# A retention layer and its gated unit: query blocks kept four tokens per partition, and another order in the first slots

## The chip, the cores and the metric

The kernel runs on one core of a Trainium2 chip. The metric is the time of one execution on the device in microseconds (us). The core has five engines that each work through their own list of instructions: TensorE (PE; its weight loads are shown as PEld), VectorE (DVE), ScalarE (ACT), GpSimd (POOL) and SyncE (SP), which issues nearly all transfers (DMA). An engine that waits for a semaphore holds up all that stands behind it in its list.

## The reference

```python
# attention-like part, B, H, S, D = 8, 8, 576, 64
scores = scale * np.matmul(q, k.transpose(0, 1, 3, 2))
Dmat = np.where(rel >= 0, gamma[:, None, None] ** rel[None, :, :], 0.0)   # rel = pos_i - pos_j
x = np.matmul(scores * Dmat[None], v)            # then heads side by side: [B, S, 512]
# gated part, K = 5
gate_pre = sum over k of conv_w[k] * xp[:, k:k + S, :]      # causal, along the tokens
gate = 1.0 / (1.0 + np.exp(-gate_pre))
out = (gate * (x @ w_val)) @ w_out
```

Inputs and output are float32.

## The kernel before

The decay gamma^(i-j) is split into a factor of the key's token and one of the query's. So the work runs in chunks of 128 tokens of one batch, all heads at once: scores of the chunk against itself under a causal mask, plus a state carried from the chunks before it. A batch has four such chunks and a tail of 64 tokens; two tails make one chunk. In all there are 36 chunks: 16 of batches 0 to 3, two of their tails, then the same for batches 4 to 7.

Lines 426 to 483 are a software pipeline written out by hand, a loop over slots t from -2 to 37. Slot t holds work of several chunks and emits it in a fixed order on every engine: the loads of chunk t+6; the casts to bf16 of chunk t+4 (keys `kb`, values `vb`, POOL) and of the query blocks to be turned in slot t+2 (`qb`, POOL); `take_state(t)` (ACT); `scores(t+1)` (PE) and the two `masks` (DVE, from PSUM to `p0`, `p1`); `values(t)` (PE); `take_x(t)` (DVE, L310), which multiplies the result `o` in PSUM by the query factor `gout` and writes it to `xg` in SBUF; `turn_k(t+2)`, four transposes on PE into the one PSUM tile `tps`, copied out by DVE as `kt`; `turn_q`, the same for queries, copied out by ACT (L244); and `carried(t+1)` and `update(t+1)`, the products with the state and into it.

Two chunks make a unit n of the gated part. In slot 2n+2 stand `conv(n)` (40 matmuls, L362), its sigmoid (ACT) and `value(n, .)`; in slot 2n+3 `project(n, .)`, whose output ACT copies (L390) and SP sends out (L393, L396). So a convolution marks the start of every even slot from slot 2 on.

Queries come in two forms. For batches 0 and 1 (`FIRST = 2`) and for the tails, each chunk's queries are a transfer of their own (`fqc`, 256 KB). For batches 2 to 7 one transfer of 1 MB brings all 512 queries of a batch with four consecutive tokens in each partition (`fqb`), which gives runs of 1 KB in HBM where the others have 256 bytes. Such a batch is turned in four blocks r = 0 to 3: block r holds tokens r, r+4, r+8 and so on. L240 puts the tokens back in order, by writing the block with a step of four elements into `qtb`. A table (L400 to L420) says in which slot which block is turned and when a batch's block is loaded.

SP issues in program order, so an output that isn't ready holds up the loads behind it. The loads of chunks 0 to 5 and the weights stand ahead of the loop (L99 to L111).

Of the kernel before, what the change touches and what calls it, by code (L numbers as in the profile page):

```python
# [13 lines left out]
F32 = mybir.dt.float32  # L14
# [7 lines left out]
def kernel(  # L22
# [22 lines left out]
    FIRST = 2  # L45
# [26 lines left out]
    with tc.manual_schedule():  # L72
# [13 lines left out]
        def load(t):  # L86
            kind, b, c = chunks[t]
            load_one("k", k, kind, b, c, LA + 1)
            if kind == "tail" or b < FIRST:
                load_one("q", q, kind, b, c, LA)  # L90
            load_one("v", v, kind, b, c, LA + 1)
# [9 lines left out]
        load(0)  # L101
# [8 lines left out]
        for t in range(3, LA - 2):  # L110
            load(t)  # L111
# [19 lines left out]

        tok = consts.tile([P, NCH + 1], F32, name="tok")
# [15 lines left out]
        warm = consts.tile([P, 1], F32, name="warm")  # L148
        nc.scalar.activation(warm, lsc, AF.Sigmoid)
# [4 lines left out]
        for t in sbd + sbl:  # L154
            nc.vector.memset(t, 0.0)
        xg = [xp.tile([P, GB, NP, PAD + S], BF16, name=f"xg{g}") for g in range(B // GB)]
# [24 lines left out]
        def prep_wv():  # L181

            src = wvf.rearrange("p o (pr ab hl j) -> p o pr ab hl j", pr=2, ab=2, hl=2)
            for (blk, j0, ab, hl) in ((0, 0, 0, 0), (0, 64, 1, 0), (2, 0, 1, 1), (2, 64, 0, 1)):
                nc.scalar.copy(wvb[:, :, blk:blk + 2, j0:j0 + 64], src[:, :, :, ab, hl, :])

        def prep_wo(o):
            nc.vector.tensor_copy(wob[:, o], wof[:, o])


        bf = {}

        def cast_kv(t):
            kind, b, c = chunks[t]
            kb = bfp.tile([P, H, D], BF16, name="kb")
            vb = bfp.tile([P, H, D], BF16, name="vb")
            (nc.vector if t < 2 else nc.gpsimd).tensor_copy(kb, loaded["k", kind, b, c])  # L197
            nc.gpsimd.tensor_tensor(vb, loaded["v", kind, b, c],  # L198
                                    gin[:, c, :].unsqueeze(2).to_broadcast([P, H, D]), op=ALU.mult)
            bf[t] = (kb, vb)  # L200
# [4 lines left out]
        def cast_q(job):  # L205
            qb = bfp.tile([P, H, D], BF16, name="qb")
            if job[0] == "own":
                kind, b, c = chunks[job[1]]
                src = loaded["q", kind, b, c]
            else:  # L210
                src = loaded["qb", job[1]][:, :, job[2], :]
            nc.gpsimd.tensor_copy(qb, src)  # L212
            qbf[job] = qb

        def turned(src):
            ps = ps_t.tile([P, NP, P], BF16, name="tps")
# [7 lines left out]
        def turn_k(t):  # L224
            ps = turned(bf[t][0])
# [4 lines left out]
        def turn_q(job, eng=None):  # L230
            ps = turned(qbf[job])
# [281 lines left out]
```

## Time and profile before

| | us |
|---|---|
| three runs | 186.19, 186.20, 213.15 |
| median | 186.2 |
| the profiled execution | 186.13 |
| its span (first to last instruction) | 184.1 |
| busy PE, DVE, ACT, POOL | 150.5, 116.3, 104.6, 79.8 |
| bytes moved, HBM read and written | 30.42 MB, 9.44 MB |

The rows in the next sections come from one profiled execution. The slices give each engine's busy share of a fortieth of the span (4.6 us) in tenths. A row of a timeline has the start, the duration, the engine, the line, the operation with output and inputs, how many instructions were merged (x) and, in brackets, how long the engine was idle before it and what ended that. A row of groups has the count, the busy time, the mean duration in ns, and the idle time before the group with what ended most of it. A row of windows has for each engine the busy time in that stretch, then TensorE's granted clock, the share of busy DMA engines (which can exceed 1, since transfers of several packets are counted while they are open) and the rate in GB/s. A piece of the chain of waits is a start, a length and what ran.

### The profile page before, as it was taken

The numbers are of one execution on the slowest core, as the hardware profiler recorded it, in microseconds if no ns is written. First come the engines' busy times: TensorE is split into PE (matmuls) and PEld (weight loads), VectorE is DVE, ScalarE is ACT, GpSimd is POOL, SyncE is SP. The second block draws the span as 40 slices with busy tenths as digits, with TensorE's granted clock in tenths as the row PEclk, the third lists the DMA queues.
The fourth block names the chain that finished last, engine by engine and source line by source line (L and its number), as shares of the span: only waits on it lengthen the run. The fifth ranks groups of instructions, "written<-read, shape, count | busy, mean of one in ns | idle before, by whom it ended". The sixth has DMA issues, their size and how long they took to land.

```text
span 184.1 us, 5545 instructions
## 1 busy us (share of the span) xinstructions
PE 150.5 (82%) x2255; PEld 113.1 (61%) x2273; DVE 116.3 (63%) x227; ACT 104.6 (57%) x182; POOL 79.8 (43%) x118
## 2 busy tenths in 40 slices
PE   0172529059999999999999999999999999999960
PEld 0151416046768686777868677686867768677630
DVE  7364527016576677777677876767787678876320
ACT  6606203206876786686755668687766764455330
POOL 4333041088684347632575157443684451710000
PEclk9999999859999999999999999999999999999997
DMA  6997999989999999999999899999999987923215
GB/s 134 219 304 183 220 218 220 306 187 251 213 270 276 251 256 237 242 230 227 249 255 270 232 237 279 255 214 231 252 271 221 240 219 174 270 80 116 76 39 116
DMA packets 100199, 40.21 MB, mean 218 GB/s; under 512 B 88378, under 2 KB 94542, under 8 KB 100174
## 3 DMA queue, kind: packets, MB, share of 16 engines
q1 hardware_dynamic: 100144, 39.86, 91.3%
q8 instruction: 17, 0.28, 0.7%
q14 instruction: 8, 0.07, 0.1%
q10 hardware_dynamic: 30, 0.01, 0.0%
HBM read 30.42 MB, written 9.44 MB: 217 GB/s over the span
## 4 chain that ended last, share of the span: by engine, by line
PE 61%; SPq 17%; DVE 7%; ACT 7%; DMA 3%; issue 2%; POOL 0%; DVEq 0%; ACTq 0%
PE g L387 16%; PE g L377 15%; SPq L79 14%; PE g L362 11%; PE tps L219 8%; ACT qtb L244 6%; DVE p L269 5%; PE s L260 5%; PE o L301 4%; DMA fqc<-in_q_dram 3%; DVE z L380 3%; PE st L329 2%; SPq L109 1%; PE o L284 1%; SPq L95 1%
## 5 line engine op out<-in xcount | busy, mean ns | idle before, releaser
L269 DVE TENSOR_TENSOR p<-s,mask 128x512 bf16<-128x512 f32 x64 | 43.9, 685 | 16.2 <-PE s L260 15.1
L198 POOL TENSOR_TENSOR vb<-fvc,gin 128x512 bf16<-128x512 f32 x36 | 37.5, 1042 | 14.1 <-DMA fvc<-in_v_dram 10.6
L377 PE MATMUL g<-xg,wvb 128*128 128x256 bf16 x288 | 38.1, 278 | 0.0
L380 DVE TENSOR_TENSOR z<-gate,g 128x512 bf16<-128x512 f32 x36 | 24.7, 687 | 20.3 <-PE g L377 20.3
L390 ACT COPY ob<-g 128x512 f32<-128x512 f32 x36 | 22.2, 618 | 24.6 <-PE g L387 24.6
L244 ACT COPY qtb<-tps 128x512 bf16<-128x512 bf16 x24 | 31.5, 1314 | 5.0 <-PE tps L219 5.0
L387 PE MATMUL g<-wob,z 128*128 128x512 bf16 x126 | 32.9, 379 | 1.4 <-DVE z L380 0.5
L197 POOL CAST kb<-fkc 128x512 bf16<-128x512 f32 x34 | 20.8, 613 | 28.3 <-DMA fkc<-in_k_dram 15.5
L219 PE MATMUL tps<-ident,kb 128*128 128x128 bf16 x144 | 15.3, 233 | 20.4 <-POOL kb L197 14.7
L377 PEld LDWEIGHTS <-wvb 128*128 128x128 bf16 x288 | 27.4, 100 | 3.4 <-issue 0.4
L370 ACT ACTIVATE gate<-g 128x512 f32<-128x512 f32 x36 | 19.5, 595 | 14.0 <-PE g L362 14.0
L227 DVE COPY kt<-tps 128x512 bf16<-128x512 bf16 x36 | 15.3, 424 | 16.7 <-PE tps L219 16.5
L219 PEld LDWEIGHTS <-kb 128*128 128x128 bf16 x144 | 8.9, 102 | 25.8 <-POOL kb L197 15.5
L362 PE MATMUL g<-xg,dg 64*64 64x256 bf16 x720 | 24.2, 279 | 0.0
L310 DVE TENSOR_TENSOR xg<-o,gout 128x512 bf16<-128x512 f32 x32 | 21.8, 680 | 0.0
L362 PEld LDWEIGHTS <-dg 64*64 64x64 bf16 x720 | 19.0, 109 | 2.3 <-issue 0.6
L212 POOL CAST qb<-fqc 128x512 bf16<-128x512 f32 x12 | 7.3, 610 | 30.1 <-DMA fqc<-in_q_dram 28.4
L340 ACT CAST sbd<-st 64x256 bf16<-64x256 f32 x48 | 17.8, 371 | 2.7 <-PE st L329 2.2
L387 PEld LDWEIGHTS <-z 128*128 128x128 bf16 x144 | 12.6, 98 | 10.3 <-DVE z L380 1.2
L212 POOL CAST qb<-fqb 128x512 bf16<-128x512 f32 x24 | 14.6, 610 | 8.5 <-DMA fqb<-in_q_dram 8.4
L219 PE MATMUL tps<-ident,qb 128*128 128x128 bf16 x144 | 14.9, 231 | 2.0 <-DVE kt L227 1.6
L244 ACT COPY qt<-tps 128x512 bf16<-128x512 bf16 x10 | 5.9, 588 | 17.9 <-PE tps L219 17.9
(52 smaller groups left out, 139.6 us busy)
## 6 DMA issues: line engine op xcount, KB each, us to landing
fkc<-in_k_dram SPq DMA_DIRECT2D x32, 256.0 KB, 5.2
fvc<-in_v_dram SPq DMA_DIRECT2D x32, 256.0 KB, 5.5
out_dram<-ob SPq DMA_DIRECT2D x32, 256.0 KB, 3.7
fqb<-in_q_dram SPq DMA_DIRECT2D x6, 1024.0 KB, 7.9
fqc<-in_q_dram SPq DMA_DIRECT2D x8, 256.0 KB, 6.4
wvf<-in_moe_w_val_dram SPq DMA_DIRECT2D x1, 1024.0 KB, 8.4
wof<-in_moe_w_out_dram SPq DMA_DIRECT2D x4, 256.0 KB, 4.8
fkc<-in_k_dram SPq DMA_DIRECT2D x8, 128.0 KB, 3.6
```

Source lines behind the costliest of these rows:

```text
L79: nc.sync.dma_start(out=t, in_=src[b, :, c * P:(c + 1) * P, :].rearrange("h p d -> p h d"))
L198: nc.gpsimd.tensor_tensor(vb, loaded["v", kind, b, c], gin[:, c, :].unsqueeze(2).to_broadcast([P, H, D]), op=ALU.mult)
L212: nc.gpsimd.tensor_copy(qb, src)
L219: nc.tensor.transpose(ps[:, pr, :], flat[:, pr * P:(pr + 1) * P], ident)
L244: nc.scalar.copy(dst, ps)
L269: nc.vector.tensor_tensor(p, sps[t][i], m.unsqueeze(1).to_broadcast([P, NP, P]), op=ALU.mult)
L310: nc.vector.tensor_tensor(x[:, bl, :, PAD + i0:PAD + i0 + P], ops[t], gout[:, :, i0:i0 + P], op=ALU.mult)
L362: nc.tensor.matmul(g[bank][cols, pr, :], lhsT=dg[rows, blk, kk, :], rhs=xs(n, rows, blk, kk), start=(pr == 0 and kk == 0), stop=(pr == 1 a ...
L377: nc.tensor.matmul(vps[:, j, :], lhsT=wvb[:, o, 2 * i + j, :], rhs=xs(n, slice(0, P), o, PAD), start=(j == 0 and o == 0), stop=(j == 1 and ...
L380: nc.vector.tensor_tensor(z, gsb[n][i], vps, op=ALU.mult)
L387: nc.tensor.matmul(o, lhsT=zsb[n, j // 2][:, j % 2, i * P:(i + 1) * P], rhs=wob[:, j, :], start=(j == 0), stop=(j == NP - 1))
L390: nc.scalar.copy(ob, o)
```

## The change

All eight batches now take the form with four tokens per partition, and the step of four is no longer undone when the queries are copied out of PSUM. `qtb` keeps the blocks side by side, `[P, NP, RQ, P]`. A chunk's 128 queries are then 32 columns of each of the four blocks, so that the columns of the scores and of `o` stand in the order (r, n) for token 4n + r. Three places answer to that: `queries` returns the four runs of 32, the mask is copied once with its columns in that order (`mask_q`), and `take_x` reads `o` with a step of 32 columns to write `xg` in token order.

```diff
-                    qtd["batch", b] = tp_sb.tile([P, NP, RQ * P], BF16, name="qtb", bufs=2)
-                dst = qtd["batch", b].rearrange("p o (n r) -> p o r n", r=RQ)[:, :, r, :]
+                    qtd["batch", b] = tp_sb.tile([P, NP, RQ, P], BF16, name="qtb", bufs=2)
+                dst = qtd["batch", b][:, :, r, :]
...
+    def queries(t, rows, pr):
+        if kind == "tail":
+            return qtd["own", t][rows, pr, :]
+        return qtd["batch", b][rows, pr, :, c * P // RQ:(c + 1) * P // RQ]
...
+        nc.gpsimd.tensor_copy(mask_q.rearrange("p (r n) -> p n r", r=RQ), mask.rearrange("p (n r) -> p n r", r=RQ))
...
-                nc.vector.tensor_tensor(x[:, bl, :, PAD + i0:PAD + i0 + P], ops[t], gout[:, :, i0:i0 + P], op=ALU.mult)
+                by_token = lambda a: a.rearrange("p o (n r) -> p o n r", r=RQ)
+                nc.vector.tensor_tensor(by_token(x[:, bl, :, PAD + i0:PAD + i0 + P]),
+                                        ops[t].rearrange("p o (r n) -> p o n r", r=RQ),
+                                        by_token(gout[:, :, i0:i0 + P]), op=ALU.mult)
```

The rest reorders the first slots. Batch 0's block is loaded right after chunk 0's keys, batch 1's after chunk 3. Batch 0 is cast (POOL and DVE in turn) and turned in slot -2, batch 1 as a whole in slot 2, batch 2 from slot 3 on, one block a slot. Keys are cast in slot t for chunk t+3, values for t+2, query blocks for slot t+1. In slots 1 to 3 `turn_k` and `turn_q` come after the value products and projections, and ACT and DVE copy the turned blocks in turn. The weight casts move: half of `w_val` to POOL (slot -1), half to ACT in slot 1; `w_out` to ACT and DVE at the end of slot 2. The memsets of `sbl` and the load of the sigmoid table move into slot -2. At the end one of the last four output transfers is issued by ACT.

```diff
-        load(0)
+        load_one("k", k, *chunks[0], LA + 1)
+        load_queries(0)
+        load_one("v", v, *chunks[0], LA + 1)
         load(1)
...
-        for t in range(3, LA - 2):
+        load(3)
+        load_queries(1)
+        for t in range(4, LA - 2):
             load(t)
...
-            for job in qjobs.get(t + 2, []):
+            if ok(t + 2) and t == -1:
+                cast_k(t + 2)
+            if ok(t + 2):
+                cast_v(t + 2)
+            if t == -1:
+                prep_wv(g_copy, 0)
+            if ok(t + 3):
+                cast_k(t + 3)
+            for job in qjobs.get(t + 1, []):
                 cast_q(job)
-            if ok(t + 4):
-                cast_kv(t + 4)
...
+            if ok(t + 2) and 1 <= t <= 3:
+                turn_k(t + 2)
+                for i, job in enumerate(jobs):
+                    turn_q(job, v_copy if i % 2 else s_copy)
...
-                    nc.sync.dma_start(out=out[b + 2 * i + j, NCH * P:S, :], in_=ob[j * TAIL:(j + 1) * TAIL])
+                    (nc.scalar if last and j else nc.sync).dma_start(out=out[b + 2 * i + j, NCH * P:S, :], in_=ob[j * TAIL:(j + 1) * TAIL])
```

On SP, the queue of the loads, from the keys of chunk 4 to those of chunk 7 (fkc keys, fqc a chunk's queries, fvc values, fqb a batch's queries; the numbers are buffers). Before:

```order
L79 DMA fkc_129<-in_k_dram 128x8x64
L79 DMA fqc_131<-in_q_dram 128x8x64
L79 DMA fvc_133<-in_v_dram 128x8x64
L79 DMA fkc_135<-in_k_dram 128x8x64
L79 DMA fqc_137<-in_q_dram 128x8x64
L79 DMA fvc_139<-in_v_dram 128x8x64
L95 DMA fqb_290<-in_q_dram 128x8x256
L79 DMA fkc_292<-in_k_dram 128x8x64
L79 DMA fqc_294<-in_q_dram 128x8x64
L79 DMA fvc_296<-in_v_dram 128x8x64
L95 DMA fqb_358<-in_q_dram 128x8x256
L79 DMA fkc_360<-in_k_dram 128x8x64
```

And after, the same stretch with batch 1's block ahead of it:

```order
L94 DMA fqb_123<-in_q_dram 128x8x256
L78 DMA fkc_125<-in_k_dram 128x8x64
L78 DMA fvc_127<-in_v_dram 128x8x64
L78 DMA fkc_129<-in_k_dram 128x8x64
L78 DMA fvc_131<-in_v_dram 128x8x64
L94 DMA fqb_287<-in_q_dram 128x8x256
L78 DMA fkc_289<-in_k_dram 128x8x64
L78 DMA fvc_291<-in_v_dram 128x8x64
L94 DMA fqb_340<-in_q_dram 128x8x256
L78 DMA fkc_342<-in_k_dram 128x8x64
```

The reads of 256 KB for queries are gone from the stretch; batch 1's block stands ahead of chunk 4, and the blocks of batches 2 and 3 (fqb_287, fqb_340) stand where they stood.

On POOL, from the casts of chunk 4 on (kb, vb, qb the cast keys, values and queries). Before:

```order
L212 CAST qb_298<-fqc_131 128x512
L212 CAST qb_300<-fqb_290 128x512
L197 CAST kb_302<-fkc_129 128x512
L198 TENSOR_TENSOR vb_303<-fvc_133,gin_164 128x512
L212 CAST qb_366<-fqc_137 128x512
L212 CAST qb_368<-fqb_290 128x512
L197 CAST kb_370<-fkc_135 128x512
```

And after:

```order
L197 CAST kb_348<-fkc_125 128x512
L215 CAST qb_350<-fqb_123 128x512
L215 CAST qb_352<-fqb_123 128x512
L215 CAST qb_354<-fqb_123 128x512
L215 CAST qb_356<-fqb_123 128x512
L202 TENSOR_TENSOR vb_405<-fvc_127,gin_158 128x512
L197 CAST kb_407<-fkc_129 128x512
L215 CAST qb_409<-fqb_287 128x512
L497 COPY maskt_192<-mask_150 128x128
L498 MEMSET maskt_192 64x64
L202 TENSOR_TENSOR vb_555<-fvc_131,gin_158 128x512
L197 CAST kb_557<-fkc_289 128x512
```

The first cast of batch 2's block stood ahead of chunk 4's keys (kb_302) and now stands behind chunk 5's (kb_407), ahead of chunk 5's values and chunk 6's keys. The four casts of batch 1's block stand between the keys and the values of chunk 4.

More of the change, by code (lines that the diff above doesn't have):

```diff
@@ L266, in masks @@
         def masks(t, i):
-            m = mask if chunks[t][0] == "full" else mask_t
+            m = mask_q if chunks[t][0] == "full" else mask_t
             p = pp.tile([P, NP, P], BF16, name=f"p{i}")
@@ L279, in carried @@
             ops[t] = o
-            qt = queries(t)
+            rows = slice(0, P)
             if kind == "full":
@@ L430 @@
             jobs = qjobs.get(t, [])
+            if t == -2:
+                cast_k(0)
+                turn_k(0)
+                for s in sbl:
+                    nc.vector.memset(s, 0.0)
+                for r in range(RQ):
+                    cast_q(("batch", 0, r), nc.vector if r % 2 else nc.gpsimd)
+                cast_v(0)
+                for r in range(RQ):
+                    turn_q(("batch", 0, r), s_copy if r % 2 else v_copy, ps_g if r < 3 else None)
+                warm = consts.tile([P, 1], F32, name="warm")
+                nc.scalar.activation(warm, lsc, AF.Sigmoid)
+                continue
             for b in qload.get(t, []):
@@ L453 @@
                 gate(n, 1)
-            if ok(t + 2):
+            if ok(t + 2) and not 1 <= t <= 3:
                 turn_k(t + 2)
```

133 lines of the change are left out of this document (56 added, 77 removed).

## The prediction, made before the changed kernel ran

> **What bounds the kernel now.** I read the 40 slices first, then the busy time by windows.
>
> ```profile
> PE   0172529059999999999999999999999999999960
> DMA  6997999989999999999999899999999987923215
> ```
>
> ```profile
> core 0: us, PE busy (x) PEld busy (x) DVE busy (x) ACT busy (x) POOL busy (x), PEclk, DMA share, GB/s
> 35.00:40.00 5.00, 1.27 (x9) 1.02 (x10) 0.42 (x1) 0.00 (x0) 2.49 (x4) 0.52 0.97 181
> 45.00:50.00 5.00, 4.92 (x85) 3.50 (x84) 3.65 (x7) 4.20 (x8) 3.26 (x7) 1.00 0.85 186
> 70.00:80.00 10.00, 9.87 (x149) 7.32 (x148) 7.18 (x12) 7.35 (x12) 5.61 (x8) 1.00 0.99 232
> 90.00:100.00 10.00, 9.95 (x158) 7.95 (x156) 7.22 (x14) 5.90 (x11) 6.28 (x9) 1.00 0.99 249
> 100.00:110.00 10.00, 9.60 (x152) 7.12 (x151) 8.00 (x15) 6.38 (x11) 4.42 (x6) 1.00 0.95 243
> ```
>
> There are two stages. Up to about 39 us TensorE is mostly idle and the DMA engines are busy: the first slots wait for data. From 40 us on TensorE is 96 to 99% busy, and DMA runs at a share near 1 beside it. So a late start is paid in full at the end, and a faster start is only kept as long as the transfers keep up. The timeline of the start shows which transfer is waited for.
>
> ```profile
> 25.57 1.14 SPq L79 DMA_DIRECT2D fkc<-in_k_dram  x1
> 26.75 1.14 SPq L79 DMA_DIRECT2D fqc<-in_q_dram  x1
> 28.51 0.61 POOL L212 CAST qb<-fqc 128x512 bf16<-128x512 f32 x1 [1.44 <-DMA fqc<-in_q_dram]
> 37.51 0.61 POOL L212 CAST qb<-fqb 128x512 bf16<-128x512 f32 x1 [8.38 <-DMA fqb<-in_q_dram]
> 38.06 0.61 POOL L197 CAST kb<-fkc 128x512 bf16<-128x512 f32 x1
> 38.73 0.61 PE L219 MATMUL tps<-ident,kb 128*128 128x128 bf16 x4 [6.71 <-POOL kb L197]
> 51.27 1.05 POOL L198 TENSOR_TENSOR vb<-fvc,gin 128x512 bf16<-128x512 f32 x1 [0.49 <-DMA fvc<-in_v_dram]
> ```
>
> In slot 2 TensorE waits 6.71 us for the cast of chunk 4's keys. The keys are there, but on POOL that cast is queued behind the first cast of batch 2's queries, which waits 8.38 us for a 1 MB transfer. From landing to the transposes it takes 38.73 - 38.06 = 0.67 us. In steady work the program repeats in units of two slots, one gate convolution each:
>
> ```profile
> 72.53 1.29 PE L362 MATMUL g<-xg,dg 64*64 64x256 bf16 x40
> 77.31 0.40 PE L219 MATMUL tps<-ident,kb 128*128 128x128 bf16 x4
> 80.49 1.29 PE L362 MATMUL g<-xg,dg 64*64 64x256 bf16 x40
> ```
>
> A unit takes 7.96 us; the odd slot turns its keys 4.8 us after the convolution starts, and 3.2 us before the next one.
>
> **The change, part by part.**
>
> *Loads and casts of the first slots.* I pace the one queue by these rows. SP's issues follow each other at 1.18 us per 256 KB. Between the casts at 28.51 and 37.51 there land v4, k5, q5, v5 and the 1 MB block: 9.00 - 4 x 1.18 = 4.28 us for the block. As a check, from 37.51 eight 256 KB reads and one block give 37.51 + 9.44 + 4.28 = 51.2, and v8's cast starts at 51.27. On this pace k7 lands in the old order at 37.51 + 4 x 1.18 + 4.28 = 46.5. In the new one the seven reads q0 to q6 ahead of it (8.26 us) are gone and two blocks (8.56 us) came instead: 46.8. So the bytes ahead of slot 5 do not arrive sooner; what changes is what TensorE has done by then. Batch 2's first block lands at 46.8 - 3 x 1.18 - 4.28 = 39.0, as late as before (37.5), but the program now asks for its cast (qb_409) after kb of chunk 5 and turns it last in slot 3. Slot 2, the value products, both projections and slot 3's work run before it, in the time in which TensorE stood still. After 39.0 + 0.67 about three small groups (an update, scores, values) stand before the second convolution, at about 41 to 43 us, and slot 5 then reaches its keys before they are there. It goes on when chunk 7 is cast: 46.8 + 0.67 = 47.5, and the third convolution starts 3.2 us later, at 50.7. Before:
>
> ```profile
> 56.60 1.22 PE g L362 x40
> 104.39 1.24 PE g L362 x39
> 120.42 1.22 PE g L362 x40
> ```
>
> That is 5.9 us earlier at that place. The low clock of 35 to 40 us (0.52, so up to 5 x 0.48 = 2.4 us of work) will fall somewhere in slots 2 to 4. The wait for chunk 7 covers part of it, and the transfers, below, leave only 3.8 of 5.9 + 1.2 us of lead, so up to 3.3 us may be lost at the start without a price at the end.
>
> The new waits: SP's block for batch 3 (fqb_340) waits for POOL's four casts of batch 1, with k7 and v7 queued behind it. Four casts at 0.56 us from start to start follow chunk 4's keys, which land near 31 us, so they end near 34; the block's turn on the engines begins at 46.8 - 1.18 - 4.28 = 41.3. Hidden by 7 us; without that cover each us would delay k7 by one. On POOL v5 and k6 are queued behind the wait for batch 2's block; v5 is used at the end of slot 4, some 5 us later. Keys are cast one slot sooner than needed instead of two, which matters only where a transfer is late (next). The weight casts that go to POOL and ACT, the memsets and the copied mask run while the start waits for data, all within the idle time seen above: nothing.
>
> *What the transfers give back.* Two later casts of keys wait for their own transfer:
>
> ```profile
> 105.58 0.61 POOL L197 CAST kb<-fkc 128x512 bf16<-128x512 f32 x1 [3.76 <-DMA fkc<-in_k_dram]
> 121.87 0.61 POOL L197 CAST kb<-fkc 128x512 bf16<-128x512 f32 x1 [3.02 <-DMA fkc<-in_k_dram]
> ```
>
> They are chunks 21 and 25, turned 4.8 us after the convolutions at 104.39 and 120.42: at 109.2 and 125.2. Less 0.67 us, the keys have 3.0 and 2.7 us to spare. If these landings do not move, TensorE can be at most 2.7 us ahead at the second place, whatever the start gained. If the queue packed without end, nothing would be given back. The windows say which end is nearer: the DMA share leaves 0.15 x 5 + 0.01 x 10 + 0.01 x 10 + 0.05 x 10 = 1.45 us idle between 45 and 110, less the 0.3 us by which k7 is later: 1.1 us. I take 2.7 + 1.1 = 3.8 us as what is left of the lead at chunk 25, the gains of the next part up to there included.
>
> *Queries in token order.*
>
> ```profile
> L244 ACT COPY qtb<-tps 128x512 bf16<-128x512 bf16 x24 | 31.5, 1314 | 5.0 <-PE tps L219 5.0
> L244 ACT COPY qt<-tps 128x512 bf16<-128x512 bf16 x10 | 5.9, 588 | 17.9 <-PE tps L219 17.9
> L310 DVE TENSOR_TENSOR xg<-o,gout 128x512 bf16<-128x512 f32 x32 | 21.8, 680 | 0.0
> L314 DVE TENSOR_TENSOR xg<-o,gout 128x256 bf16<-128x256 f32 x8 | 3.0, 414 | 0.0
> 100.47 0.40 PE L260 MATMUL s<-qtb,kt 64*128 64x128 bf16 x8 [0.29 <-ACT qtb L244]
> ```
>
> The copy no longer scatters its output, so it falls from 1314 to about 588 ns. That takes 24 x 0.73 = 17 us off ACT, which is no bound. On the path it removes the wait of the first scores of each of batches 2 to 7, 0.29 us where it is shown: 6 x 0.29 = 1.7 us, of which two (0.6 us) come after chunk 25. The other copies are hidden by TensorE. The scores and carried products now read four runs of 32 queries in place of one of 128. The nearest row is the convolution at 104.39, of the tails: it reads four runs of 64 where that at 120.42 reads one of 256, and takes 1.24 against 1.22 us. So 0.02 us for 40 instructions is the upper end, 0.01 us for the unit's 24, 0.2 us in all; nothing is the lower one, and I take it, since the bound of 0.02 is within what such rows vary.
>
> The price is on DVE, where the 32 full takes of x (L310) now read PSUM with 128 bytes between neighbours. No row shows such a read. Half the elements take 414 ns and all 680, so an element costs 1.04 ns. The ends are 680 ns (free) and, by the scattered copy's ratio 1314/588, 1520 ns. I take 680: the scattered row is a write of two-byte elements on another engine, and L314, a read of the same tile in separate runs, pays nothing. Below 680 there is no reason to go. This is the least certain term.
>
> [...]
>
> *The end.* The last output goes out as four issues on SP:
>
> ```profile
> 178.31 2.44 SPq L396 DMA_DIRECT2D out_dram<-ob  x4
> L396 SPq DMA_DIRECT2D out_dram<-ob x8: 522/588/2967, 117.2 to 180.2; - x8
> ```
>
> The last of them moves to ACT's queue, beside its sister: one issue, about 0.5 us.
>
> *Sum.* The profiled execution took 186.13 us, of which 184.1 are the span and 2.03 lie around it; the median shown is 186.2, the same. 3.8 (lead left at chunk 25) + 0.6 (two waits after it) + 0.5 (the end) = 4.9 us: 186.1 - 4.9 = 181.2 us.
>
> **The rivals.**
>
> *1. The strided take costs one more step per element:* 680 + 512 x 1.04 = 1210 ns. The even slot then holds TensorE:
>
> ```profile
> 72.89 0.68 DVE L310 TENSOR_TENSOR xg<-o,gout 128x512 bf16<-128x512 f32 x1
> 74.18 0.42 DVE L227 COPY kt<-tps 128x512 bf16<-128x512 bf16 x1
> 74.86 0.39 PE L219 MATMUL tps<-ident,qb 128*128 128x128 bf16 x4
> 69.90 0.68 DVE L310 TENSOR_TENSOR xg<-o,gout 128x512 bf16<-128x512 f32 x1
> 70.50 0.68 DVE L269 TENSOR_TENSOR p<-s,mask 128x512 bf16<-128x512 f32 x1
> 71.85 0.40 PE L260 MATMUL s<-qtb,kt 64*128 64x128 bf16 x8
> ```
>
> The key copy would end at 74.60 + 0.53 = 75.13, and the query transposes at 74.86, which need its PSUM tile, would wait about 0.3 us in each unit. Of the 15 units from the third on, nine lie before chunk 25, so the lead there is 5.9 + 1.2 - 2.7 = 4.4, still cut to 3.8; the other six cost 1.8: 181.2 + 1.8 = 183.0 us. For it: strides do cost in this trace (1314 against 588). Against it: they cost on a write. [...]
>
> *2. The take costs what the scattered copy does, 1520 ns: slower than before.* The even slot waits 0.58 + 0.05, and in the odd slot the second mask ends at 71.18 + 0.84 = 72.0, after the scores at 71.85 that need its tile: 0.2 more. 15 x 0.83 = 12.5 us against 5.9 + 1.7 + 0.5 = 8.1 gained, and no transfer is late any more: 186.1 + 4.4 = 190.5. It passes the slower mark of 2% (189.9) from a take of about 1.48 us on.
>
> *3. The transfers take back more:* the earlier outputs push the inputs, and chunk 25 lands as before or later. With no earlier landing the lead is 2.7 and the time 182.3; up to 2 us later, 184.3. For it: a DMA share of 0.95 to 1 in every window. Against it: the share measures open packets, and the rate in these windows varies from 232 to 249 GB/s, so there may be room.
>
> *4. Nothing is given back:* 186.1 - 8.1 = 178.0.
>
> **How the numbers follow.** Forecast with free strides 0.55 (rival 4, as its low edge, within it), rival 1 0.2, rival 2 0.1, rival 3 0.15. The likeliest gives 181.2. 2% (about what a measurement of this kernel tells from no change) lies at 182.5 and 189.9. Faster: 0.48 of the forecast's 0.55, 0.05 of rival 1, 0.03 of rival 3: 0.56; slower: rival 2, 0.1; the rest, 0.34, within. The range 178.3 to 185.0 leaves out rival 2 and the outermost edges of the others. The forecast's own range is 178.3 to 182.6.
>
> **What would show it.** The strided take's mean: 680 ns, or 1.2 or 1.5 us. The query copy's mean near 590 ns. No wait of 6 us for a key cast; the second convolution near 42, the third near 51, with a wait for chunk 7 before it. Chunks 21 and 25: key casts that end a wait for DMA with TensorE waiting behind them; if TensorE does not wait there, rival 4 holds. A convolution period above 8 us without waits for casts means the take. I am wrong altogether if TensorE idles before 39 us on something other than data, or if k7 lands well after 47.

## The result, and the profile after

The changed kernel took 179.47 us as the median of four executions (177.41 to 181.30), against 186.19 before; the ratio is 0.957, with a 95% interval of 0.948 to 0.967, about 178.2 us. Run once more beside the kernel before on another occasion it took 178.62 (178.34 to 179.57) against 185.85: 0.962 (0.959 to 0.966). It is faster by 7 to 8 us, where 4.9 were forecast. Ratios leave disturbed executions out; the first profiled one (180.25 us) was such, so the lines below are those of the repeat, profiled at 178.34 us with a span of 176.4.

> The changed kernel once more, so that the next three have it beside them on the same chip. Theory T: the start gains about 6.3 us at the third convolution, later transfers take back little (one stall of TensorE of about 1.4 us for the keys of chunk 21), and the waits for query copies (1.7 us) are gone: 178 us, against 186.2 before. Rival P (the prediction's term): the landings of chunks 21 and 25 cap the lead at 2.7 us plus 1.1 us, TensorE stands still for over 2.5 us there in all, and the time is 181. A second profile also says whether the stall for chunk 21 is the same from run to run.

The slices of the repeat, 4.4 us each:

```profile
PE   0277179489999999999999789998999999999980
DMA  5999999989989999989999999999999997863114
```

The two stages are still there, but TensorE is full from about 40 us on, and a dip has come in the 23rd and 24th slice, near 100 us. In the chain of waits, a piece is a start, a length and what ran; first the repeat, then the kernel before:

```profile
39.93 1.22 PE g L365 x40
47.97 1.22 PE g L365 x40
...
105.40 1.22 PE g L365 x40
113.22 1.22 PE g L365 x40
...
166.28 1.24 PE g L365 x39
```

```profile
47.99 1.22 PE g L362 x40
...
112.45 1.22 PE g L362 x38
...
173.11 1.24 PE g L362 x39
```

The third convolution comes at 47.97 against 56.60: a lead of 8.6 us. At the tenth it is 112.45 - 105.40 = 7.05, at the last 173.11 - 166.28 = 6.8, and on the span 184.1 - 176.4 = 7.7. So the lead is made at the start, 1.6 us of it go between 96 and 106 us, and the end adds 0.9. The timeline of TensorE shows what it waits for:

```profile
23.03 0.61 PE L222 MATMUL tps<-ident,kb 128*128 128x128 bf16 x4 [4.61 <-POOL kb L197]
31.43 0.38 PE L222 MATMUL tps<-ident,qb 128*128 128x128 bf16 x4 [0.96 <-DVE kt L230]
32.48 0.38 PE L222 MATMUL tps<-ident,qb 128*128 128x128 bf16 x4 [0.67 <-ACT qtb L244]
33.38 0.38 PE L222 MATMUL tps<-ident,qb 128*128 128x128 bf16 x4 [0.51 <-DVE qtb L244]
34.44 0.38 PE L222 MATMUL tps<-ident,qb 128*128 128x128 bf16 x4 [0.67 <-ACT qtb L244]
...
101.93 0.40 PE L222 MATMUL tps<-ident,kb 128*128 128x128 bf16 x4 [1.57 <-POOL kb L197]
123.06 0.40 PE L222 MATMUL tps<-ident,kb 128*128 128x128 bf16 x4 [0.58 <-POOL kb L197]
```

The wait of 6.71 us in slot 2 is gone. What is left there are four short waits (2.8 us), since the keys of chunk 4 and the four blocks of batch 1 go one after the other through one PSUM tile and TensorE waits for each copy. The wait of 1.57 us at 101.93 is for chunk 21, the one of 0.58 us at 123.06 for chunk 26. The cast of chunk 21 waited for its transfer, as the timeline of POOL shows:

```profile
43.60 0.61 POOL L197 CAST kb<-fkc 128x512 bf16<-128x512 f32 x1 [3.03 <-DMA fkc<-in_k_dram]
101.26 0.61 POOL L197 CAST kb<-fkc 128x512 bf16<-128x512 f32 x1 [4.39 <-DMA fkc<-in_k_dram]
117.12 0.61 POOL L197 CAST kb<-fkc 128x512 bf16<-128x512 f32 x1 [3.08 <-DMA fkc<-in_k_dram]
```

These are chunks 7, 21 and 25. The last two are cast 4.3 and 4.75 us earlier than before (105.58, 121.87), and TensorE does not wait for chunk 7 or for chunk 25. The groups:

```profile
L311 DVE TENSOR_TENSOR xg<-o,gout 128x512 bf16<-128x512 f32 x32 | 21.8, 681 | 0.0
L244 ACT COPY qtb<-tps 128x512 bf16<-128x512 bf16 x27 | 15.9, 588 | 9.7 <-PE tps L222 9.7
```

The strided take of x costs 681 ns, where the plain one cost 680; the query copy fell from 1314 to 588.

### The profile page after: what moved, and what is told of

Same layout as the page of the kernel before. It is cut to its first block, busy times and chain, and to the rows that moved or that the text cites. A ratio compares the mean times of both kernels' runs of the same rounds, so it can differ in the third digit from the quotient of the medians.

```text
span 177.4 us, 5549 instructions
## 1 busy us (share of the span) xinstructions
PE 151.7 (86%) x2273; PEld 112.2 (63%) x2273; DVE 117.7 (66%) x229; ACT 88.4 (50%) x180; POOL 81.6 (46%) x119
## 3 DMA queue, kind: packets, MB, share of 16 engines
q1 hardware_dynamic: 93744, 39.59, 90.9%
HBM read 30.42 MB, written 9.44 MB: 225 GB/s over the span
## 4 chain that ended last, share of the span: by engine, by line
PE 74%; DMA 9%; SPq 8%; DVE 2%; POOL 2%; ACT 1%; issue 1%; ACTq 0%; DVEq 0%; POOLq 0%
PE g L391 17%; PE g L380 17%; PE g L365 12%; PE tps L222 10%; DMA fkc<-in_k_dram 9%; PE o L301 6%; PE s L260 6%; SPq L78 4%; PE st L332 4%; SPq L110 3%; PE o L284 3%; POOL kb L197 1%; DVE z L383 1%; ACT qtb L244 1%; ACT ob L394 1%
## 5 line engine op out<-in xcount | busy, mean ns | idle before, releaser
L269 DVE TENSOR_TENSOR p<-s,maskq 128x512 bf16<-128x512 f32 x64 | 43.9, 685 | 15.6 <-PE s L260 15.4
L391 PE MATMUL g<-wob,z 128*128 128x512 bf16 x144 | 37.5, 389 | 0.3 <-DVE z L383 0.3
L380 PE MATMUL g<-xg,wvb 128*128 128x256 bf16 x288 | 36.9, 274 | 0.0
L394 ACT COPY ob<-g 128x512 f32<-128x512 f32 x36 | 21.1, 586 | 28.9 <-PE g L391 28.6
L380 PEld LDWEIGHTS <-wvb 128*128 128x128 bf16 x288 | 26.8, 98 | 3.5 <-issue 0.8
L215 POOL CAST qb<-fqb 128x512 bf16<-128x512 f32 x30 | 18.7, 632 | 7.1 <-DMA fqb<-in_q_dram 7.1
L244 ACT COPY qtb<-tps 128x512 bf16<-128x512 bf16 x27 | 15.9, 589 | 8.7 <-PE tps L222 8.7
L222 PEld LDWEIGHTS <-qb 128*128 128x128 bf16 x144 | 11.3, 103 | 11.6 <-POOL qb L215 4.2
L222 PE MATMUL tps<-ident,qb 128*128 128x128 bf16 x132 | 13.0, 222 | 3.3 <-DVE kt L230 1.5
L301 PE MATMUL o<-p,vb 128*64 128x128 bf16 x288 | 15.8, 235 | 0.0
```

Of the source, the lines that this page charges most:

```text
L222: nc.tensor.transpose(ps[:, pr, :], flat[:, pr * P:(pr + 1) * P], ident)
L269: nc.vector.tensor_tensor(p, sps[t][i], m.unsqueeze(1).to_broadcast([P, NP, P]), op=ALU.mult)
L301: nc.tensor.matmul(o[r, pr, :], lhsT=vb[:, 2 * pr + i, :], rhs=pt[t, i][:, pr, :], start=(fresh and pr == 0), stop=(pr == NP - 1), skip_gr ...
L380: nc.tensor.matmul(vps[:, j, :], lhsT=wvb[:, o, 2 * i + j, :], rhs=xs(n, slice(0, P), o, PAD), start=(j == 0 and o == 0), stop=(j == 1 and ...
L391: nc.tensor.matmul(o, lhsT=zsb[n, j // 2][:, j % 2, i * P:(i + 1) * P], rhs=wob[:, j, :], start=(j == 0), stop=(j == NP - 1))
L394: nc.scalar.copy(ob, o)
```

## The experiments

All ratios are to the kernel before, run on the same chip beside each.

| kernel | us, median | ratio | 95% |
|---|---|---|---|
| changed kernel, repeat | 178.62 | 0.962 | 0.959 to 0.966 |
| start order alone | 182.23 | 0.982 | 0.977 to 0.987 |
| token order alone | 183.51 | 0.989 | 0.985 to 0.993 |
| two blocks in 256-byte runs | 180.96 | 0.975 | 0.971 to 0.979 |
| all blocks in 256-byte runs | 191.93 | 1.027 | 1.022 to 1.033 |
| all blocks in four transfers, 1 KB runs | 179.36 | 0.966 | 0.962 to 0.971 |
| a quarter of the output | 176.83 | 0.954 | 0.950 to 0.957 |
| before, a quarter of the output | 185.94 | 1.004 | 1.001 to 1.007 |
| w_out late | 178.27 | 0.959 | 0.954 to 0.963 |
| keys first | 178.58 | 0.959 | 0.954 to 0.965 |
| keys first and w_out late | 180.19 | 0.966 | 0.960 to 0.972 |
| start order alone, more tiles | 179.19 | 0.965 | 0.959 to 0.970 |
| changed kernel, more tiles | 177.19 | 0.956 | 0.952 to 0.959 |
| the same, keys first | 179.12 | none | |

**The two parts, each alone.** The start order with the scattered copy put back:

```diff
-                dst = qtd["batch", b][:, :, r, :]
+                dst = qtd["batch", b].rearrange("p o (n r) -> p o r n", r=RQ)[:, :, r, :]
...
-            return qtd["batch", b][rows, pr, :, c * P // RQ:(c + 1) * P // RQ]
+            return qtd["batch", b][rows, pr, c * P:(c + 1) * P]
...
-            m = mask_q if chunks[t][0] == "full" else mask_t
+            m = mask if chunks[t][0] == "full" else mask_t
```

> The new order of the first slots alone: all queries in blocks with four tokens per partition, but put back in token order by the scattered copy, plain mask, plain take of x, scores that read one run of 128 columns. Theory T: the query copies on ACT take 1.31 us again, DVE's scattered copies at the start somewhat less or more, and each batch from 2 on waits about 0.3 us for its first scores: 178 + 1.7 = about 180 us, with the third convolution at 50 to 52 us. Rival P: transfers cap the lead at 2.7 to 3.8 us, so the 1.7 us are paid only after chunk 25 (0.6 us): 181 to 182 us, close to the changed kernel. Rival A (the token order is worth much more than its waits, because ACT's 17 us hold something else up): 183 us or more.

And the reverse, the token order for batches 2 to 7 in the kernel before:

```diff
-                dst = qtd["batch", b].rearrange("p o (n r) -> p o r n", r=RQ)[:, :, r, :]
+                dst = qtd["batch", b][:, :, r, :]
...
+            m = mask_t if chunks[t][0] != "full" else mask if ("own", t) in qtd else mask_q
```

> The token order alone, in the kernel before: batches 2 to 7 keep their four-token order through scores, mask and take of x; batches 0 and 1 keep their own loads, plain mask and plain take; order of the first slots as before. Theory T: the six waits of 0.29 us go, 186.2 - 1.7 = 184.5 us; the strided take is 0.68 us like the plain one beside it in the same kernel. Rival A: 183 us or less. Rival C (the copies are hidden anyway, or the four runs of 32 cost TensorE what the waits gave): 186.2 us.

182.23 and 183.51 us: 3.6 and 2.3 us gained, 5.9 in all where both together gain 7.2. The first is near rival P's time, but not for its reason: TensorE does not wait for keys there after 40 us. The groups of the second kernel hold both takes of x side by side, strided (L317) and plain (L314):

```profile
L317 DVE TENSOR_TENSOR xg<-o,gout 128x512 bf16<-128x512 f32 x24 | 16.3, 681 | 0.0
L314 DVE TENSOR_TENSOR xg<-o,gout 128x512 bf16<-128x512 f32 x8 | 5.5, 682 | 0.0
```

In the start order alone, slot 2 is longer. The timeline of TensorE, then the groups of copies:

```profile
33.91 0.38 PE L219 MATMUL tps<-ident,qb 128*128 128x128 bf16 x4 [1.38 <-ACT qtb L241]
35.67 0.38 PE L219 MATMUL tps<-ident,qb 128*128 128x128 bf16 x4 [1.38 <-DVE qtb L241]
```

```profile
L241 ACT COPY qtb<-tps 128x512 bf16<-128x512 bf16 x27 | 35.5, 1314 | 9.8 <-PE tps L219 9.8
L241 DVE COPY qtb<-tps 128x512 bf16<-128x512 bf16 x2 | 2.6, 1298 | 4.7 <-PE tps L219 4.7
```

The waits between blocks are 1.38 us in place of 0.51 to 0.67. So the two parts are not independent: the fast copy shortens a chain that only the new start order has. But the waits are not all of it, since TensorE's granted clock was low there, as the windows of this kernel and then of the repeat show:

```profile
35.00:40.00 5.00, 2.40 (x26) 1.91 (x27) 2.56 (x4) 2.96 (x5) 3.40 (x7) 0.66 1.07 271
40.00:45.00 5.00, 4.26 (x28) 2.16 (x28) 3.38 (x5) 1.17 (x2) 3.00 (x4) 0.65 1.28 245
```

```profile
35.00:40.00 5.00, 4.36 (x62) 2.77 (x63) 3.55 (x8) 3.13 (x8) 3.54 (x7) 1.00 0.92 229
40.00:45.00 5.00, 4.95 (x93) 4.21 (x89) 4.05 (x8) 2.71 (x6) 1.97 (x4) 1.00 0.98 212
```

The second convolution comes at 45.88 against 39.93, 5.95 us later. Of these, 0.7 us stand already when chunk 4's keys are turned (30.80 against 30.08) and 2.3 us come with the waits up to the fourth block (37.44 against 34.44). The other 2.95 come mostly in the stretch with the low clock: from the fourth block to chunk 5's keys the same work takes 43.70 - 37.44 = 6.26 us, against 37.75 - 34.44 = 3.31, and only 0.54 of the 6.26 are a wait for the last copy.

To take the waits out, batch 1 was turned through more PSUM tiles, scattered copies and all:

```diff
-                    turn_q(job, v_copy if i % 2 else s_copy)
+                    turn_q(job, v_copy if i % 2 else s_copy, ps_g if job[1] == 1 and i < 3 else None)
```

> The start order alone again (scattered copies, 182.2 us), but the four blocks of batch 1 are turned in slot 2 through three PSUM tiles of another pool and one of the old, in place of one tile four times. Theory W (the token order is worth 1.3 to 1.9 us more in the changed kernel than its six waits, because in slot 2 TensorE waits for each copy before it can turn the next block, 1.38 us each with the scattered copy against 0.5 to 0.7): TensorE's waits of 1.38 us in slot 2 fall below 0.5 us each, the second convolution comes about 2 to 3 us earlier than 45.8, and the time falls to about 180.5. Rival A (ACT's longer copies cost somewhere in the steady slots): the waits in slot 2 go, but the time stays at 182.2 within 0.7.

The waits between the turned blocks fell to 0.16 us, and the time from 182.23 to 179.19, more than expected, with copies that still take 1.31 us. The waits are on the path, as theory W has it; for ACT's 17 us in the steady slots nothing speaks. But the low clock went with the waits: the mean granted clock of the six executions is 0.964 to 0.980 in the start order alone and 0.991 to 1.000 here. How the 3.0 us divide between the two, and whether the waits bring the low clock, no run shows. Now TensorE reaches chunk 7 before its keys, as its timeline shows:

```profile
43.60 0.40 PE L219 MATMUL tps<-ident,kb 128*128 128x128 bf16 x4 [1.11 <-POOL kb L194]
...
47.00 1.29 PE L359 MATMUL g<-xg,dg 64*64 64x256 bf16 x40
...
103.55 0.40 PE L219 MATMUL tps<-ident,kb 128*128 128x128 bf16 x4 [3.08 <-POOL kb L194]
```

The third convolution is bound by that landing, 3.4 us ahead of it, and the larger lead is paid back at chunk 21 with 3.08 us.

**The price of a block.** The blocks of batches 0 and 1, then of all eight, were loaded in runs of 256 bytes:

```diff
-            nc.sync.dma_start(out=t.rearrange("p h r d -> p h (r d)"),
-                              in_=q[b, :, 0:RQ * P, :].rearrange("h (p r) d -> p h (r d)", r=RQ))
+            if b < 2:
+                for r in range(RQ):
+                    nc.sync.dma_start(out=t[:, :, r, :],
+                                      in_=q[b, :, 0:RQ * P, :].rearrange("h (p r) d -> p h r d", r=RQ)[:, :, r, :])
+            else:
+                nc.sync.dma_start(out=t.rearrange("p h r d -> p h (r d)"),
+                                  in_=q[b, :, 0:RQ * P, :].rearrange("h (p r) d -> p h (r d)", r=RQ))
```

> The changed kernel with the query blocks of batches 0 and 1 loaded by four transfers each, one for each block r, so that they are read in runs of 256 bytes in place of 1 KB: the same bytes, the same tiles, the same order. Theory R (the transfers gave back less than predicted because 1 KB runs take less time of the DMA engines): two blocks cost 8 x 1.18 = 9.4 us in place of 2 x about 3.3, so the landings of chunks 4, 7 and 21 move back by about 2.8 us and the time rises by 2 to 3 us, to 181. Rival S (the pace of the queue does not depend on the runs, and the lead is only what the order of the first slots gains): the time stays at 178.6 within 0.7.

> The same for the query blocks of all eight batches. Theory R: each of the other six costs 4 x 1.18 - 3.3 = 1.4 us more of a queue that is nearly full (share near 1 after 45 us), so up to 8.4 us more on top of the run with two: between 183 and 189, with TensorE waiting for casts of keys at several places in each half. Rival S: 178.6 to 179.5.

That makes four issues out of one, so a control splits the block by heads and keeps the runs at 1 KB:

```diff
-            nc.sync.dma_start(out=t.rearrange("p h r d -> p h (r d)"),
-                              in_=q[b, :, 0:RQ * P, :].rearrange("h (p r) d -> p h (r d)", r=RQ))
+            for j in range(0, H, 2):
+                nc.sync.dma_start(out=t[:, j:j + 2].rearrange("p h r d -> p h (r d)"),
+                                  in_=q[b, j:j + 2, 0:RQ * P, :].rearrange("h (p r) d -> p h (r d)", r=RQ))
```

> The control for the run with all eight blocks in runs of 256 bytes (191.9): the blocks are again loaded by four transfers each, but split by heads, two heads at a time, so that the runs stay at 1 KB. Theory R (the length of the runs sets the price): 178.6 within 0.7. Rival I (the number of issues or of transfers sets it): 188 to 192.

180.96, 191.93 and 179.36 us. The control's interval overlaps the repeat's, so it is the run length and not the number of transfers. The rows of the queue on the page (packets, MB, share of 16 engines' span), for the repeat, for all blocks in short runs, and for the control:

```profile
q1 hardware_dynamic: 93744, 39.59, 91.8%
```

```profile
q1 hardware_dynamic: 118704, 39.59, 92.8%
```

```profile
q1 hardware_dynamic: 94128, 39.59, 90.8%
```

The same 39.59 MB take 0.918 x 176.4 = 161.9 us, 0.928 x 189.4 = 175.8 and 0.908 x 176.4 = 160.2. The short runs cost 13.9 us for eight blocks, 1.7 each, and the time rises by about as much: 191.9 - 178.6 = 13.3 us by the medians, about 12 by the ratios, more than the 183 to 189 us expected. This queue is the bound that the lead runs into. The casts of chunk 4 give a second reading, first the repeat, then all blocks in short runs, then two:

```profile
27.82 0.61 POOL L197 CAST kb<-fkc 128x512 bf16<-128x512 f32 x1 [3.31 <-DMA fkc<-in_k_dram]
```

```profile
33.21 0.61 POOL L202 CAST kb<-fkc 128x512 bf16<-128x512 f32 x1 [5.86 <-DMA fkc<-in_k_dram]
```

```profile
32.05 0.61 POOL L202 CAST kb<-fkc 128x512 bf16<-128x512 f32 x1 [5.83 <-DMA fkc<-in_k_dram]
...
105.46 0.61 POOL L202 CAST kb<-fkc 128x512 bf16<-128x512 f32 x1 [4.46 <-DMA fkc<-in_k_dram]
122.70 0.61 POOL L202 CAST kb<-fkc 128x512 bf16<-128x512 f32 x1 [4.27 <-DMA fkc<-in_k_dram]
```

Two blocks lie ahead of it, so a block costs (33.21 - 27.82) / 2 = 2.7 us more, or (32.05 - 27.82) / 2 = 2.1. In the run with two blocks, chunk 7 is cast at 47.38 in place of 43.60, and chunks 21 and 25 (the last two rows) about where they were in the kernel before. Its profiled execution (183.4 us) was well above its median, so its later rows are weak evidence.

The change itself can be read on the page in the same way. The first row is the kernel before, the second the queue of ACT in the repeat, where two output transfers have gone:

```profile
q1 hardware_dynamic: 100144, 39.86, 91.3%
```

```profile
q10 hardware_dynamic: 190, 0.27, 0.6%
```

The queue took 0.913 x 184.1 = 168.1 us before and 161.9 in the repeat, of which 0.006 x 176.4 = 1.1 us moved to ACT's. So giving eight reads of 256 KB for two blocks took 168.1 - 161.9 - 1.1 = 5.1 us off the transfers.

**What is given back.** The output cut to a quarter, in the changed kernel and in the one before:

```diff
-                nc.sync.dma_start(out=out[b, c0:c0 + P, :], in_=ob)
+                nc.sync.dma_start(out=out[b, c0:c0 + P, 0:DM // 4], in_=ob[:, 0:DM // 4])
```

> The changed kernel with only the first 128 of 512 columns of each full chunk's output sent out (the tails' outputs are whole): 6.3 MB of 40.2 MB fewer to move. Theory T (what is given back is given back to a full queue): TensorE's waits for the casts of keys at chunk 21 and after it (2.2 us in the profile of the repeat) are gone, the order at the start is as before, and the time falls by about 2 us, to 176.5. Rival Q (the stall at chunk 21 is not the transfers' rate but the order of work on POOL or SP): it stays, and the time stays within 0.7 of 178.6.

> The control: the kernel before with the same three quarters of the full chunks' output left unsent. Theory T: TensorE never waits there for keys after 45 us, so the time changes by less than 0.7 us from 185.9. Rival (transfers slow TensorE in other ways, or the first slots run on less crowded queues): over 1.5 us faster.

176.83 us, without a wait for keys after 40 us, and 185.94, no gain. So the late keys are the price of a full queue (its packets took 91.8% of the span in the repeat, 84.6% with a quarter of the output), and it is only paid once TensorE is ahead. With nothing given back, the chain of the changed kernel with a quarter of the output also measures the steady part of the change:

```profile
47.87 1.22 PE g L365 x40
...
163.29 1.24 PE g L365 x40
```

From the third convolution to the last: 115.42 us, against 173.11 - 56.60 = 116.51 before, 1.1 us less. The start order alone, with the scattered copies, takes 170.44 - 53.92 = 116.52, and the kernel before with a quarter of the output 172.77 - 56.25 = 116.52, so the 1.1 us belong to the token order.

Then the queue was put in another order, a chunk's keys and values ahead of the same slot's block:

```diff
-            for b in qload.get(t, []):
+            late = t > 0
+            for b in qload.get(t, []) if not late else []:
                 load_queries(b)
             if t >= 0 and ok(t + LA - 2):
                 load(t + LA - 2)
+            for b in qload.get(t, []) if late else []:
+                load_queries(b)
```

> The changed kernel with one swap on the queue of the loads: from slot 1 on, a chunk's keys and values are issued ahead of the 1 MB block of queries of the same slot (the keys are cast two slots earlier than the block). Nothing else moves. Theory T (the stall is a full queue with a block of about 3.3 us ahead of the keys of chunk 21): the keys land about 3 us earlier, before 99 us, TensorE's wait there of 1.4 to 1.6 us goes, and the time falls from 178.6 to about 177, as with a quarter of the output (176.8). Rival Q (the queue is late as a whole; the block then comes late instead): TensorE waits for query casts in place of keys, and the time stays at 178.6.

Chunk 21 was cast at 97.09 and TensorE did not wait for it, but for two others (0.67 us at 89.66, 0.42 at 105.83), and the median did not move. Next, w_out was loaded later, first alone and then together with keys first:

```diff
-        for (p0, blk, ab, hl) in ((0, 0, 0, 0), (64, 0, 1, 0), (0, 2, 1, 1), (64, 2, 0, 1)):
-            nc.sync.dma_start(out=wof[p0:p0 + 64, blk:blk + 2, :], in_=wo_src[ab, hl])
         load(3)
         load_queries(1)
-        for t in range(4, LA - 2):
+        load(4)
+        for (p0, blk, ab, hl) in ((0, 0, 0, 0), (64, 0, 1, 0), (0, 2, 1, 1), (64, 2, 0, 1)):
+            nc.sync.dma_start(out=wof[p0:p0 + 64, blk:blk + 2, :], in_=wo_src[ab, hl])
+        for t in range(5, LA - 2):
             load(t)
```

> The changed kernel with the 1 MB load of w_out moved behind chunk 3, batch 1's queries and chunk 4, so that TensorE's wait of 4.87 us for the keys of chunk 3 shrinks by 3 to 4 us. Theory T (little is taken back): the first convolution near 23 us, the third near 47.5 (bound by the keys of chunk 7, which land at 43.3 as before), and the time falls by about 2 to 3 us, to 175 to 176. Rival P (the transfers cap the lead): the gain at the start appears, and comes back as longer stalls for the keys of chunk 21 (about 1.4 + 3 us) and later ones, at 178 us as the changed kernel.

> The swap of keys and query block together with w_out loaded behind chunk 4. Theory T: with the keys of chunk 7 no longer behind batch 3's block they land 3 us earlier, so the early gain of the late w_out (first convolution near 23 us) can reach the third convolution, below 46 us against 47.9 in the repeat, and little of it is taken back: 175 us. Rival P (the queue as a whole bounds slots 3 to 6): no better than the swap alone, 177.

The late w_out (178.27) can't be told from the repeat, and with keys first it was 180.19; the expected 175 to 176 came in neither. Their profiled executions were over 182 us, well above their medians, so where the early gain goes is not settled by them. Last, the line for more tiles, shown above, was put into the changed kernel and into the one with keys first:

> The changed kernel with batch 1 turned in slot 2 through three PSUM tiles of another pool and one of the old, as in the run before this one. Theory T: TensorE's waits of 0.96, 0.67, 0.51 and 0.67 us in slot 2 go, the third convolution comes at 47 us (the keys of chunk 7, landing near 43, bound it), and about 1 us is left at the end: 177.5 us against 178.6. Rival P (whatever the start gains beyond this, the waits for the keys of chunks 21 and after take back): 178.6, with more than 3 us of such waits.

> The same, and from slot 1 on a chunk's keys and values are issued ahead of the same slot's block of queries. Theory T (the order of the queue takes the lead back): chunk 7's keys land 3 us earlier, so the third convolution can come before 46 us, the waits for keys of chunks 21 and after stay below 1.5 us, and the time is 176 to 176.5. Rival P (the queue's rate takes it back): 178 to 178.6, and the waits only move to other chunks.

More tiles in the changed kernel gave 177.19, with no execution above 178.4: the best kernel of the study by about 1 us, its interval just touching the repeat's. Its waits, in the timeline of TensorE:

```profile
45.26 0.40 PE L222 MATMUL tps<-ident,kb 128*128 128x128 bf16 x4 [1.82 <-POOL kb L197]
...
101.91 0.40 PE L222 MATMUL tps<-ident,kb 128*128 128x128 bf16 x4 [1.03 <-POOL kb L197]
```

Here is the wait for chunk 7 that the prediction described. With keys first as well the executions scattered from 175.61 to 180.45, too far for a ratio, and the waits of the profiled one stood at other chunks (2.41 us at 90.75). A new order moves the waits; a gain from it is not shown.

## Why the prediction fell short

**The bound and the place: right.** A late start paid in full at the end, the third convolution as the place, chunk 21 as the place where transfers take back. No rival of the slower side was near.

**The price of the added blocks: the step that failed.** The text took 4.28 us for a block of 1 MB from an interval between two casts, 28.51 to 37.51, and put it on the two blocks that the change adds, those of batches 0 and 1. So it had chunk 4's keys land near 31 and chunk 7's at 46.8. Both casts ended a wait for their transfer, at 27.82 and 43.60: 3.2 us early, and all of that ahead of chunk 4. In the kernel before, chunk 4's queries landed at 28.51 and its keys, one read ahead, at about 28.51 - 1.18 = 27.33. Four reads fewer and two blocks more moved them by 0.5 us, which makes (4 x 1.18 + 0.5) / 2 = 2.6 us for a block (an estimate; the start varies, and other kernels with these loads have that cast at 27.5 to 29.3, so up to 3.3). The queue's rows give (8 x 1.18 - 5.1) / 2 = 2.2 us. The short runs give 4 x 1.18 less 2.7 or 2.1 by the landings, 2.0 to 2.6, and less 1.7 as the mean of all eight blocks, 3.0, if a quarter of a block in short runs costs 1.18 us as other reads do; no run shows that by itself.

At 4.28 the change saved nothing on the queue (seven reads of 8.26 us against two blocks of 8.56); at 2 to 3 us the eight reads of batches 0 and 1 (9.44) become 4 to 6, and 3.4 to 5.4 us of transfers are gone for good. With the two blocks in short runs the kernel does what was forecast: 180.96 us against 181.2, chunk 7 cast at 47.38 against 46.8 landed.

Later in the start the price held: from chunk 4's cast to chunk 7's there are six reads and the blocks of batches 2 and 3, in 43.60 - 27.82 = 15.78 us, 4.35 a block, where the text had 46.8 - 31 = 15.8. Its check to 51.27 was sound too, but it read such a later block once more and said nothing of those loaded in the first 27 us. Why a block costs less there no run isolates.

In runs of 256 bytes the same 8 MB of queries took 13.9 us more of the queue than in runs of 1 KB (175.8 against 161.9 us); what lengths between the two cost no run shows. The size of a transfer made no difference for these loads: in four transfers of 256 KB, with runs of 1 KB, the queue took 160.2 us, and in one of 1 MB 161.9.

**What the transfers give back: mis-sized by the same step.** The text kept chunks 21 and 25 within 1.1 us of their old landings and so cut the lead to 3.8 us. They were cast 4.3 and 4.75 us earlier, and 7.2 us of lead stood at the convolution ahead of chunk 25 (120.42 - 113.22). Chunk 21 cost 1.57 us, chunk 25 nothing. The 1.1 us came from the idle share of the DMA engines, which cannot show that the queue has less to move. With the two blocks in short runs the two casts are at 105.46 and 122.70, near their old places (105.58, 121.87), and TensorE waits 1.43 and 1.32 us for them, as the text had it. Rival 4 (nothing given back, 178.0) came nearest in time by luck: the run with a quarter of the output is still 1.8 us faster than the repeat, so something is given back, and the gains are larger than rival 4 had them.

**The third convolution: 2.7 us too late, by the same step.** 50.7 was forecast, 47.97 measured. With the landing at 43.60 the text's own rule gives 43.60 + 0.67 + 3.2 = 47.5. The wait for chunk 7 that should have set it was not there: TensorE turned these keys at 44.51, just after they were cast, held in slot 2 by the turns through one tile. That chain is a term that the text left out ("The other copies are hidden by TensorE"); in the repeat it is 2.8 us. The first profile has the third convolution at 50.31, near the forecast, for another reason: its start was later and its granted clock was 0.66 from 35 to 40 us.

**The low clock: open.** The text let it fall somewhere in slots 2 to 4, hidden in part. In the repeat's profile it did not come; in the start order alone the stretch under it took 6.26 - 0.54 - 3.31 = 2.4 us longer, its wait left out, which is an estimate of what it cost of the lead there. What brings it no run isolates. The kernel before with a quarter of the output waits 6.02 us in slot 2, and its mean granted clock is 0.999, so one long wait came without it.

**The token order: right in place, 1.1 for 1.7 us** in the steady slots. Six periods between convolutions got shorter, one for each of batches 2 to 7: five by about 0.15 us and only the one with the wait at 100.47 by 0.35. The text took the one wait that the trace shows for all six. Alone in the kernel before it gave 2.3 (ratio 0.985 to 0.993), but not all of that is its own. From the third convolution to the last its profile is 116.51 - (170.68 - 54.91) = 0.7 us shorter; the rest stands before, where the first block of batch 2 was cast 1.4 us earlier (36.13 against 37.51). The kernel before with a quarter of the output, which loads that block in the same order, has this cast at 36.44, so the start varies by about as much.

**The strided take: right.** 681 ns beside 682 in one kernel; rivals 1 and 2 are out. On this read, of fp32 in PSUM with 128 bytes between neighbours, the step adds no time.

**The end: 0.9 us for 0.5.** From the last convolution to the end of the span, 184.1 - 173.11 = 11.0 became 176.4 - 166.28 = 10.1. The text, and the account of the change ahead of it, count one issue that moves to ACT's queue; two of the last four do, one for each half of the last unit (the timeline of ACT has them at 171.50 and 172.75).

**The waits costed at nothing** (the weight casts, the memsets, SP behind POOL's casts of batch 1) were not tested one by one. One of them shows in the repeat: POOL's cast of `w_val` waits 2.09 us for its transfer at 13.98, chunk 2's keys stand behind it, and TensorE waits 1.26 us for these at 15.85. It then waits 4.61 us for chunk 3's keys, whose cast waited for its own transfer, so that the earlier wait is covered.

In sum, against the profiled 184.1: 8.6 at the third convolution, 1.1 in the steady slots and 0.9 at the end are 10.6, and the span is 7.7 shorter. The remainder of 2.9 is what late transfers took back, and it is not measured as such: the waits for late keys are 1.57 + 0.58 = 2.15 us, and a quarter of the output gains 1.8. Forecast were 5.9, 1.2 and 0.6 before and after chunk 25, and 0.5, less 3.3 taken back: 4.9.

## What to carry to other kernels

Price a kind of transfer by the difference of two kernels, or by the queue's busy time over many of them. A price read between two landings need not hold for a transfer elsewhere in the program (here 4.28 us in one stretch against an estimated 2 to 3 in another), and a check in the same stretch cannot tell. Here, where TensorE was nearly full from 40 us on and the queue's packets took 91.8% of the span, TensorE waited 2.15 us for late keys, and with a quarter of the output not at all, so ask of a change first how much of the queue's time it removes. Where several results go through one PSUM tile in a row, the copy's duration can be on the path: in slot 2 TensorE waited 1.38 us a block behind copies of 1.31, and 0.51 to 0.67 behind copies of 0.42 and 0.59, though ACT was busy for only 59% and 50% of those spans. And look at the granted clock of both profiles before a difference is put down to waits alone.

## What the runs showed of the hardware

- A bf16 copy of 128x512 from PSUM that writes with a step of four elements took 1298 ns on VectorE and 1314 on ScalarE in the start order alone, against 424 and 588 in the repeat, where the output is contiguous; the take of x, which reads fp32 PSUM with 128 bytes between neighbours, took VectorE 681 ns against 682 without the step.
- The short runs were paid by the queue, and not by the number of issues: 8 MB in 256-byte runs took 175.8 - 160.2 = 15.6 us more of the queue than in 1 KB runs, in as many transfers.
- The first convolution took 2.35 us for 40 instructions in the repeat, against 1.29 later, under a granted clock shown as 1.00. Four transposes took 0.61 us at 23.03 and 0.38 at 31.43. The wait of 4.61 us just ahead of it is not needed for that: with `w_out` late TensorE waits 2.85 us at 17.82 and 0.55 at 21.48, and the first convolution, at 23.53, took 2.35 us as well. The cause is open.

```profile
25.53 2.35 PE L365 MATMUL g<-xg,dg 64*64 64x256 bf16 x40
39.86 1.29 PE L365 MATMUL g<-xg,dg 64*64 64x256 bf16 x40
```

- The granted clock fell in one kernel and stayed full in its neighbour: 0.66 and 0.65 from 35 to 45 us in the start order alone, 1.00 in the repeat, and a stretch of the same work took 6.26 us, 0.54 of them a wait, against 3.31.
